# Block transposes of x on VectorE and score products on sixteen array tiles

## The chip, the cores and the metric

The kernel runs on one core of a Trainium2 chip. The metric is the device time of one execution in microseconds (us), with lower being better; the time of a kernel is the median of several executions.

## The reference

Inputs are `x` (8 batches, 8 heads, 512 tokens, 64 features) and `state` (8 batches, 8 heads, 32 states, 64 features), both float32, and the float64 weights of a gated feed-forward layer. For every batch and head, tokens read from states and states read from tokens; the 512 + 32 rows of each batch, with the heads side by side, are then 544 rows of 512 features for the layer.

```python
scale = 1.0 / np.sqrt(D)
scores = scale * np.matmul(x, state.transpose(0, 1, 3, 2))
a = softmax(scores)                       # max subtracted; sum + 1e-9
xread = np.matmul(a, state)
scores2 = scale * np.matmul(state, x.transpose(0, 1, 3, 2))
a2 = softmax(scores2)
sread = np.matmul(a2, x)
rows = concatenate([xread, sread], axis=2)     # then (B*(S+Ns), H*D)

xn = rows / sqrt(mean(rows**2) + 1e-6) * rms_g
g = xn @ w_gate                                # 512 -> 1536
out = (g * sigmoid(g) * (xn @ w_val)) @ w_out  # 1536 -> 512
```

`scores2` is the transpose of `scores`, so one set of score products serves both reads.

## The kernel before, in words

**Reading (attention).** `tokens_read(b)` makes, for batch b, the weights with which tokens read states. The state of a batch lies packed in `rows`, 128 partitions of four pairs of heads times 32 states, and x in `x_b`, 128 tokens on the partitions in four chunks. TensorE turns both round with an identity (L268 for the state, L278 for x: 16 transposes of 128 by 128), VectorE copies the state's transpose out (L271) and ScalarE that of x, chunk by chunk (`xT`, L280). The score products at L287 have 64 rows (the features of one head), 32 columns of weights (its states) and 512 tokens: eight of them on eight tiles of the array, the even heads into one bank of the PSUM pool `at`, the odd ones into the other. VectorE turns the scores in blocks of 32 by 32 (L298, `eS`), takes the maximum over the states (L307), subtracts it (L309), ScalarE takes the exponential (L311), VectorE sums, divides and turns back (L318 to L325), which gives `aT_s`. ScalarE also copies the scores as they are (`sS`, L300) for `states_read(b)`, which makes the states' reads from them (L368 to L406). A product of `aT_s` with the state (L332), squares (L339), sums (L342, L346) and a power on GpSimd give the normalization of each token, and L356 scales `aT_s` by it. The tokens' reads themselves are never written: the layer's weights are multiplied by the state once for each batch (`own_weights`, L450, copied out at L461), so that the hidden layer's products take `aT_s` directly.

**The layer.** Batch 0 uses plain products (`hidden`, L492, and `project_as_ready`, L690), in step with the weights as they become ready. Batches 1 to 7 and the states use seven block products for eight (`hidden_seven`, L596; `project_seven`, L750), with sums on VectorE and GpSimd.

**The weights** come as float64, four pieces ahead (`raws`), and are turned into float32 by three ScalarE steps (L195 to L200) and four VectorE steps (L221 to L233); 18 pieces, all in the stage of batch 0. Pairs of them are stored in HBM (`w_d`) and fetched again for every batch (L148).

**Order.** The work of TensorE, VectorE and ScalarE is laid down by hand, in strings in which each letter advances one stream by one step: `ORDER` for batch 0 with the reading of batches 0 and 1, the weights and batch 0's layer; `PERIOD` for each of batches 1 to 7, with the reading of the next batch within it; `STATES` for the rows of the states. In `ORDER`, a and A are the tokens' reads of batches 0 and 1, s and S the states' reads, e and d the weights' ScalarE and VectorE steps, v the weights by the state, h, t, u the hidden layer and p its projection. In `PERIOD`, a and s are the reading of the next batch. Engines work through their instructions in this order. The DMA queues have the order in which the loads and stores are issued, nearly all on the sync queue (SPq); batch 0's x is shared between that queue and ScalarE's.

PSUM has two buffers each of `at` and `pv` for these steps; the layer has four banks of its own.

Of the kernel before, what the change touches and what calls it, by code (L numbers as in the profile page):

```python
# [8 lines left out]
F32 = mybir.dt.float32  # L9
# [10 lines left out]
W_BUFS = 3  # L20

ORDER = (
    "aaaaaaaaddaaaaaaeaseeaasadsassssdsaaaasaeadesaeeasdasaaeadeadaaaddeeasedaadsadae"
    "edvvavdadeaAhdeeddtdAdAAhueheAeedtddphAedvdvduvdphedeAedtdhApeehddeuAdddeAhdedvd"
    "tudvvpeAAAAdhdAAteAehuhpddephepdeAdAeApAdteedAAvvveAdpudAAephtdSdhAdphdeAueedhAd"
    "eAteudddeeSppAddAAdppAdAdevApvdveehhAdthAudhpdeddeedeAdteAupvdvdvphedAAtdShhutSA"
    "hpukSSSkkkwSwkpSkpwpSSckSScckkpcSwkkkwwww"
)

PERIOD = (  # L30
    "hthtvvhhtuxxhuhthuhththuuhtuuhhxxhhuvxutvhtthuuhuhthuuxhxhxuxtthuhuthhuthuxxhuta"
    "uahatuhtaxuuuhtauahuahhaahuttuhutauhhhtuuahuhuutauphuauupuauapacasapaaaapapaskaa"
    "aaksacccassppakckpaaackasaapakapaskaaaswpksksswsxxwxxpxcspcskx"
)

STATES = (
# [6 lines left out]
def kernel(  # L43
# [31 lines left out]
    SCALE = 1.0 / D ** 0.5  # L75
# [3 lines left out]
    one = ctx.enter_context(tc.tile_pool(name="one", bufs=1))  # L79
    two = ctx.enter_context(tc.tile_pool(name="two", bufs=2))  # L80
# [3 lines left out]
    aps = ctx.enter_context(tc.tile_pool(name="aps", bufs=2, space=PSUM))  # L84
    vps = ctx.enter_context(tc.tile_pool(name="vps", bufs=2, space=PSUM))
# [9 lines left out]


    rows = {}
    x_sb = {}

    def load_state(b):  # L100

        rows[b] = two.tile([P, 2, D], F32, name="rows")
        for j in range(4):
            src = state[b, 2 * j:2 * j + 2].rearrange("e n d -> n e d")
            nc.sync.dma_start(out=rows[b][Ns * j:Ns * j + Ns], in_=src)

    def load_x(b, *queues):
        x_sb[b] = two.tile([P, NC, H * D], F32, name="x_b")
        for c in range(NC):
            (queues or (nc.sync,))[c % max(1, len(queues))].dma_start(  # L110
                out=x_sb[b][:, c].rearrange("p (h d) -> p h d", h=H),
                in_=x[b, :, P * c:P * c + P, :].rearrange("h p d -> p h d"))

    ident = consts.tile([P, P], F32, name="ident")
    make_identity(nc, ident)
# [7 lines left out]
    rms_g = consts.tile([P, NI], F32, name="rms_g")  # L123
# [119 lines left out]
    stT_g = {}  # L243
    aT_s = {}
# [16 lines left out]
    read = {}  # L261

    def tokens_read(b):
        xb, packed = x_sb[b], rows.pop(b)
        stT = two.tile([P, 4, Ns], F32, name="stT")
        stT_g[b] = two.tile([P, 4, Ns], F32, name="stT_g")
        tp = aps.tile([P, 4, Ns], F32, name="at")
        TE.transpose(out=tp.rearrange("p j n -> p (j n)"),  # L268
                     in_=packed.rearrange("p e d -> p (e d)"), identity=ident)
        yield  # L270
        VE.tensor_copy(stT, tp)  # L271
        yield "step"

        xT = one.tile([P, 4, NC, P], F32, name="xT", tag="xT")
        for c in range(NC):
            tp = aps.tile([P, 4, P], F32, name="at")
            for j in range(4):
                TE.transpose(out=tp[:, j, :], in_=xb[:, c, P * j:P * j + P], identity=ident)  # L278
            yield
            SE.copy(xT[:, :, c, :], tp)  # L280
            yield "step"


        sp = [aps.tile([P, S], F32, name="at") for e in range(2)]
        for j in range(4):
            for e in range(2):
                TE.matmul(out=sp[e][Ns * j:Ns * j + Ns, :], lhsT=stT[D * e:D * e + D, j, :],  # L287
                          rhs=xT[D * e:D * e + D, j].rearrange("p c t -> p (c t)"),
                          start=True, stop=True)
        yield  # L290


        sS = read[b] = two.tile([P, 2, NC, P], F32, name="sS")
        eS = one.tile([P, 2, S // Ns, Ns], F32, name="eS", tag="eS")
        m1 = two.tile([P, 2, S // Ns], F32, name="m1")
        z1 = two.tile([P, 2, S // Ns], F32, name="z1")
        for e in range(2):
            VE.transpose(out=eS[:, e].rearrange("p k n -> p (k n)"), in_=sp[e])  # L298
            yield
            SE.copy(sS[:, e].rearrange("p c t -> p (c t)"), sp[e])  # L300
            yield "step" if e else None

        def along(t, e):
            return t[:, e].unsqueeze(2).to_broadcast([P, S // Ns, Ns])

        for e in range(2):
            VE.reduce_max(out=m1[:, e], in_=eS[:, e], axis=AXX)  # L307
            yield
            VE.tensor_tensor(out=eS[:, e], in0=eS[:, e], in1=along(m1, e), op=ALU.subtract)  # L309
            yield  # L310
            SE.activation(out=eS[:, e], in_=eS[:, e], func=ACTF.Exp, scale=SCALE)  # L311
            yield "step"
        VE.tensor_tensor(out=stT_g[b], in0=stT, in1=rms_g.unsqueeze(2).to_broadcast([P, 4, Ns]),
                         op=ALU.mult)
        yield
        aT_s[b] = two.tile([P, 2, S], F32, name="aT_s")
        for e in range(2):
            VE.reduce_sum(out=z1[:, e], in_=eS[:, e], axis=AXX)  # L318
            yield
            VE.tensor_scalar(z1[:, e], z1[:, e], 1e-9, None, op0=ALU.add)  # L320
            VE.reciprocal(z1[:, e], z1[:, e])
            yield
            VE.tensor_tensor(out=eS[:, e], in0=eS[:, e], in1=along(z1, e), op=ALU.mult)
            yield
            VE.transpose(out=aT_s[b][:, e], in_=eS[:, e].rearrange("p k n -> p (k n)"))  # L325
            yield "step"


        reads = [(aps, vps)[j // 2].tile([P, S], F32, name=("at", "pv")[j // 2]) for j in range(4)]
        for j in range(4):  # L330
            for e in range(2):
                TE.matmul(out=reads[j][D * e:D * e + D, :],  # L332
                          lhsT=packed[Ns * j:Ns * j + Ns, e, :],
                          rhs=aT_s[b][Ns * j:Ns * j + Ns, e],
                          start=True, stop=True)
        yield
        sq = one.tile([P, 4, S], F32, name="sq", tag="xT")
# [12 lines left out]
        VE.tensor_scalar(ss, sp, 1e-6, None, op0=ALU.add)  # L350
        yield "step"
        ri = mean_root(ss, NC)
        yield
        rp = along_rows(ri, NC)
        yield
        VE.tensor_tensor(out=aT_s[b], in0=aT_s[b],  # L356
                         in1=rp.unsqueeze(1).to_broadcast([P, 2, S]), op=ALU.mult)
        yield "step"

    def states_read(b):  # L360

        xb, sS = x_sb.pop(b), read.pop(b)
        e2 = one.tile([P, 2, NC, P], F32, name="e2")
        s2 = two.tile([P, 2], F32, name="s2")
        m2 = two.tile([P, 2], F32, name="m2")
        z2 = two.tile([P, 2], F32, name="z2")
        for e in range(2):
            VE.reduce_max(out=m2[:, e:e + 1], in_=sS[:, e].rearrange("p c t -> p (c t)"),  # L368
                          axis=AXX)
            yield  # L370
        VE.tensor_scalar(s2, m2, -SCALE, None, op0=ALU.mult)
        yield
        for e in range(2):
            SE.activation(out=e2[:, e], in_=sS[:, e], func=ACTF.Exp, scale=SCALE,
                          bias=s2[:, e:e + 1], accum_out=z2[:, e:e + 1])
            yield "step" if e else None
        e2T = one.tile([P, 2, NC, P], F32, name="e2T")
        for e in range(2):
            tp = aps.tile([P, NC, P], F32, name="at")
# [9 lines left out]
        for e in range(2):  # L389
            for c in range(NC):  # L390
                for j in range(4):
                    h = 2 * j + e
                    TE.matmul(out=rp[Ns * j:Ns * j + Ns, e, :],  # L393
                              lhsT=e2T[:, e, c, Ns * j:Ns * j + Ns],
                              rhs=xb[:, c, D * h:D * h + D],
                              start=(c == 0), stop=(c == NC - 1))
# [511 lines left out]
    n = B * (NM // 2)  # L908
# [37 lines left out]
```

## Time and profile before

| | |
|---|---|
| time, median of 3 | 802.42 us (801.93 to 803.89) |
| span of the profiled execution | 800.7 us |
| TensorE busy | 775.7 us, 97% |
| VectorE busy | 515.1 us, 64% |
| ScalarE busy | 347.0 us, 43% |
| GpSimd busy | 178.0 us, 22% |
| TensorE on the transposes of x (L278) | 21.0 us, 128 instructions |
| TensorE on the score products (L287) | 8.7 us, 128 instructions |
| ScalarE on the copies of x's transpose (L280) | 18.8 us, 32 instructions |
| moved by DMA | 94.11 MB, 117 GB/s from and to HBM over the span |

In the profile PE is TensorE's products, PEld its loading of weights, DVE VectorE, ACT ScalarE, POOL GpSimd, SPq the sync engine's queue of DMA issues. The page cuts the span in 40 slices of about 20 us and gives the busy share of each in tenths. A group's line names source line, engine, operation, output and inputs, shapes and count; after the first bar stand total busy time (us) and mean duration of one (ns), after the second the idle time just before them and what ended it. Durations of products overlap, so the mean of one is more than its share of the busy time. The chain of waits is followed back from the last instruction to what released each, and its pieces tell how long each group held the end back.

### The profile page before, as it was taken

How to read it: one execution, taken by the hardware profiler on the slowest of the kernel's cores; microseconds unless marked ns; L12 is line 12 of the kernel's file. 1: busy time of each engine (PE TensorE's matmuls, PEld its weight loads, DVE VectorE, ACT ScalarE, POOL GpSimd, SP SyncE). 2: the span in 40 equal slices, each digit the busy share in tenths (PEclk: the TensorE clock that was granted, in tenths of full speed). 3: DMA queues.
4: the chain of work that ended last, by engine and by line, in shares of the span. 5: the costliest groups of instructions: out<-in, count | busy, mean ns of one | idle time of the engine just before them, and what ended most of it. 6: DMA issues, size and time to landing. Idle time of an engine off the chain costs nothing.

```text
span 800.7 us, 12112 instructions
## 1 busy us (share of the span) xinstructions
PE 775.7 (97%) x4822; PEld 594.2 (74%) x4822; DVE 515.1 (64%) x786; ACT 347.0 (43%) x572; POOL 178.0 (22%) x215
## 2 busy tenths in 40 slices
PE   4599999999999999999999999999999999999998
PEld 3244444788778887888778887888788877888996
DVE  5989997588337852786358833785178735891461
ACT  5888864553145323543256314532354224510320
POOL 0000003530155004510443015500451044400000
PEclk8599999999999999999999999999999999999999
DMA  9888745710182007400361018200540024101311
GB/s 295 245 264 308 263 161 172 251 53 0 36 284 106 1 16 214 194 1 15 116 232 63 1 34 285 106 1 14 179 177 2 13 107 178 71 0 46 113 54 27
DMA packets 61592, 94.11 MB, mean 118 GB/s; under 512 B 38752, under 2 KB 46432, under 8 KB 54624
## 3 DMA queue, kind: packets, MB, share of 16 engines
q1 hardware_dynamic: 59360, 92.75, 33.5%
q8 instruction: 38, 0.62, 0.3%
q10 hardware_dynamic: 2176, 0.59, 0.3%
q14 instruction: 18, 0.15, 0.1%
HBM read 78.12 MB, written 15.20 MB: 117 GB/s over the span
## 4 chain that ended last, share of the span: by engine, by line
PE 94%; DVE 4%; ACT 1%; issue 0%; DMA 0%; SPq 0%; DVEq 0%
PE f L596 37%; PE f L750 35%; PE f L690 5%; PE pv L492 4%; PE at L450 3%; PE pv L450 3%; PE at L278 2%; PE at L332 1%; PE at L287 1%; PE at L346 1%; PE at L393 1%; PE at L381 1%; DVE ex L228 1%; DVE raw L224 1%; PE at L257 1%; DVE w_m L233 0%
## 5 line engine op out<-in xcount | busy, mean ns | idle before, releaser
L750 PE MATMUL f<-wo,hb 128*128 128x256 f32 x540 | 124.2, 382 | 0.4 <-ACT ot L787 0.2
L658 DVE TENSOR_TENSOR g<-g,f 128x512 f32<-128x512 f32 (+1 forms) x96 | 62.8, 654 | 90.0 <-PE f L596 86.6
L596 PE MATMUL f<-aT_s,v 128*128 128x256 f32 x504 | 119.5, 380 | 0.0
L750 PEld LDWEIGHTS f<-wo,hb 128*128 128x128 f32 x540 | 101.4, 190 | 20.1 <-ACT ot L787 6.9
L596 PEld LDWEIGHTS f<-aT_s,v 128*128 128x128 f32 x504 | 93.8, 190 | 17.4 <-issue 5.2
L250 POOL TENSOR_TENSOR ri<-ss,mhalf 128x4 f32<-128x4 f32 x8 | 9.1, 1142 | 364.7 <-DVE ss L350 364.7
L596 PE MATMUL f<-aT_t,vs 128*128 128x256 f32 x336 | 87.2, 382 | 0.0
L750 PE MATMUL f<-wt,hs 128*128 128x256 f32 x360 | 80.4, 379 | 0.0
L649 ACT ACTIVATE hb<-g 128x1024 f32<-128x1024 f32 (+1 forms) x48 | 48.2, 1004 | 63.0 <-DVE g L658 63.0
L750 PEld LDWEIGHTS f<-wt,hs 128*128 128x128 f32 x360 | 68.3, 190 | 9.5 <-issue 0.2
L787 ACT COPY ot<-f 128x256 f32<-128x256 f32 x60 | 21.5, 371 | 122.5 <-PE f L750 122.5
L596 PEld LDWEIGHTS f<-aT_t,vs 128*128 128x128 f32 x336 | 62.6, 190 | 15.1 <-issue 5.9
L661 DVE SCALAR_TENSOR_TENSOR hb<-hb,g 128x1024 f32<-128x1024 f32 x42 | 55.5, 1322 | 7.8 <-ACT hb L649 7.8
L647 ACT COPY g<-f 128x512 f32<-128x512 f32 (+1 forms) x48 | 26.9, 561 | 76.7 <-PE f L596 76.7
L479 POOL TENSOR_TENSOR vs<-v,vs 128x256 f32<-128x256 f32 x42 | 58.4, 1390 | 0.0
L476 POOL TENSOR_TENSOR vs<-v 128x256 f32<-128x256 f32 x42 | 30.6, 729 | 118.4 <-ACT v L461 118.4
L492 PE MATMUL pv<-aT_s,v 128*128 128x512 f32 x96 | 46.2, 623 | 1.1 <-DVE aT_s L356 1.1
L690 PE MATMUL f<-wo,hb 128*128 128x512 f32 x96 | 44.7, 600 | 0.0
L596 PE MATMUL f<-aT_t,v 128*128 128x256 f32 x168 | 43.9, 383 | 0.0
L596 PE MATMUL f<-aT_s,vs 128*128 128x256 f32 x168 | 43.1, 379 | 0.0
L750 PE MATMUL f<-wt,hb 128*128 128x256 f32 x180 | 42.6, 386 | 0.0
L750 PE MATMUL f<-wo,hs 128*128 128x256 f32 x180 | 41.6, 382 | 0.0
(128 smaller groups left out, 1237.2 us busy)
## 6 DMA issues: line engine op xcount, KB each, us to landing
w_m<-w_d SPq DMA_DIRECT2D x48, 1024.0 KB, 6.7
x_b<-in_x_dram SPq DMA_DIRECT2D x30, 256.0 KB, 4.2
out_dram<-ot SPq DMA_DIRECT2D x56, 128.0 KB, 1.8
raw<-in_moe_w_val_dram SPq DMA_DIRECT2D x6, 1024.0 KB, 5.2
raw<-in_moe_w_out_dram SPq DMA_DIRECT2D x6, 1024.0 KB, 7.2
w_d<-w_m SPq DMA_DIRECT2D x6, 1024.0 KB, 4.9
raw<-in_moe_w_gate_dram SPq DMA_DIRECT2D x5, 1024.0 KB, 5.8
raw<-in_moe_w_gate_dram SPq DMA_DIRECT2D x2, 512.0 KB, 4.9
```

The lines of the kernel that those rows point to most:

```text
L450: TE.matmul(out=pv[e][Ns * j:Ns * j + Ns, :], lhsT=stT_g[b][D * e:D * e + D, j, :], rhs=w[D * e:D * e + D, j].rearrange("p m k f -> p (m k ...
L476: GE.tensor_tensor(out=vs[:, 0], in0=a21, in1=a22, op=ALU.add)
L479: GE.tensor_tensor(out=vs[:, 2], in0=a12, in1=vs[:, 1], op=ALU.subtract)
L492: TE.matmul(out=to[0], lhsT=lhs(i, k), rhs=r, start=(i == 0), stop=(i == len(rhs) - 1))
L596: TE.matmul(out=ps[:, i, 0:half], lhsT=l[:, i, :], rhs=r, start=(start and i == 0 and k == 0), stop=(k == len(lhs) - 1), skip_group_check= ...
L647: SE.copy(gates(q)[1], q["x"][:, :, 0:half])
L649: SE.activation(out=hb[:, 2 * mp:2 * mp + 2, 0:n].rearrange("p m (c t) -> p m c t", c=2), in_=q["g"][:, :, :, 0:half], func=ACTF.Silu if s ...
L658: VE.tensor_tensor(out=to, in0=to, in1=q[ps][:, :, 0:half], op=ALU.add)
L661: VE.scalar_tensor_tensor(out=h, in0=h, scalar=1.0, op0=ALU.add, op1=ALU.mult, in1=q["g"].rearrange("p m c t -> p m (c t)"))
L690: TE.matmul(out=banks[r], lhsT=hb[:, m, P * r:P * r + P], rhs=wo[:, m, :], start=(m == 0), stop=(m == NM - 1))
L750: TE.matmul(out=banks[name][:, r, :], lhsT=lhs(k)[:, P * r:P * r + P], rhs=rhs(k), start=(start and r == 0 and k == 0), stop=(k == HM - 1) ...
L787: SE.copy(to, banks[name][:, r, :])
```

## The change

VectorE transposes in blocks of 32 by 32 take the place of TensorE's transposes of x and of their copies by ScalarE. For this x is loaded so that the 32-partition group g of a tile holds the tokens 128 g to 128 g + 127, 32 of them in each chunk. A block transpose then puts 32 features on the partitions of each group, and the 64 features of a head become two halves, k = 0 and 1, one after the other in the free dimension. The state is needed on all four groups with the same halves, so it is loaded a second time, four-fold (`fours`), and turned by VectorE as well (`stB`).

The score products then have 32 rows (half a head's features), 32 columns of weights and 128 tokens; the two halves accumulate. Token group g sets the rows of the array, pair of heads j the columns, so that sixteen tiles are in use; each group g writes a bank of its own, four in all, two from `at` and two from `pv`. What follows works on token groups (four pieces, in two halves) where it worked on even and odd heads. The packed state's transpose by TensorE stays for the weights' scaling (`stT_g`), which now reads it from PSUM. `ORDER` and `PERIOD` are new; `STATES` stays.

The aim is to take the transposes off TensorE and the copies off ScalarE.

```diff
 def load_state(b):
+        fours[b] = one.tile([P, H, D], F32, name="fours")
+        for g in range(4):
+            nc.sync.dma_start(out=fours[b][Ns * g:Ns * g + Ns],
+                              in_=state[b].rearrange("h n d -> n h d"))

 def load_x(b, *queues):
         x_sb[b] = two.tile([P, NC, H * D], F32, name="x_b")
-        for c in range(NC):
-            (queues or (nc.sync,))[c % max(1, len(queues))].dma_start(
-                out=x_sb[b][:, c].rearrange("p (h d) -> p h d", h=H),
-                in_=x[b, :, P * c:P * c + P, :].rearrange("h p d -> p h d"))
+        for i in range(4 * NC):
+            c, g = divmod(i, 4)
+            (queues or (nc.sync,))[i % max(1, len(queues))].dma_start(
+                out=x_sb[b][Ns * g:Ns * g + Ns, c].rearrange("p (h d) -> p h d", h=H),
+                in_=x[b, :, P * g + Ns * c:P * g + Ns * c + Ns, :].rearrange("h p d -> p h d"))

 def tokens_read(b):
-        VE.tensor_copy(stT, tp)
-        for c in range(NC):
-            tp = aps.tile([P, 4, P], F32, name="at")
-            for j in range(4):
-                TE.transpose(out=tp[:, j, :], in_=xb[:, c, P * j:P * j + P], identity=ident)
-            SE.copy(xT[:, :, c, :], tp)
-        sp = [aps.tile([P, S], F32, name="at") for e in range(2)]
-        for j in range(4):
-            for e in range(2):
-                TE.matmul(out=sp[e][Ns * j:Ns * j + Ns, :], lhsT=stT[D * e:D * e + D, j, :],
-                          rhs=xT[D * e:D * e + D, j].rearrange("p c t -> p (c t)"),
-                          start=True, stop=True)
-        for e in range(2):
-            VE.transpose(out=eS[:, e].rearrange("p k n -> p (k n)"), in_=sp[e])
-            SE.copy(sS[:, e].rearrange("p c t -> p (c t)"), sp[e])
+        VE.transpose(out=stB.rearrange("p h k n -> p (h k n)"),
+                     in_=fours.pop(b).rearrange("p h d -> p (h d)"))
+        n = NC if b == 0 else 2
+        for i in range(n):
+            c = slice(NC // n * i, NC // n * i + NC // n)
+            VE.transpose(out=xB[:, c].rearrange("p c h k t -> p (c h k t)"),
+                         in_=xb[:, c].rearrange("p c f -> p (c f)"))
+        sp = [(aps, vps)[g // 2].tile([P, 2, NC, Ns], F32, name=("at", "pv")[g // 2])
+              for g in range(4)]
+        for e in range(2):
+            for k in range(2):
+                for j in range(4):
+                    for g in range(4):
+                        TE.matmul(out=sp[g][Ns * j:Ns * j + Ns, e].rearrange("n c t -> n (c t)"),
+                                  lhsT=stB[Ns * g:Ns * g + Ns, 2 * j + e, k, :],
+                                  rhs=xB[Ns * g:Ns * g + Ns, :, 2 * j + e, k, :],
+                                  start=(k == 0), stop=(k == 1), skip_group_check=True)
+        for g in (2, 3, 0, 1):
+            VE.transpose(out=eS[:, g].rearrange("p e c n -> p (e c n)"),
+                         in_=sp[g].rearrange("p e c t -> p (e c t)"))
+            SE.copy(sS[:, :, :, g, :], sp[g])
...
-        VE.tensor_tensor(out=stT_g[b], in0=stT, in1=rms_g.unsqueeze(2).to_broadcast([P, 4, Ns]),
+        VE.tensor_tensor(out=stT_g[b], in0=tp, in1=rms_g.unsqueeze(2).to_broadcast([P, 4, Ns]),
                          op=ALU.mult)
...
-            VE.transpose(out=aT_s[b][:, e], in_=eS[:, e].rearrange("p k n -> p (k n)"))
+            for g in (2 * q, 2 * q + 1):
+                VE.transpose(out=aT_s[b][:, :, P * g:P * g + P],
+                             in_=eS[:, g].rearrange("p e c n -> p e (c n)"))
```

In the changed kernel's own line numbers the new transposes stand at L272 (state) and L280 (x), the products at L292, the turned scores at L305, their copies at L308, the scaling of `aT_s` at L374.

More of the change, by code (lines that the diff above doesn't have):

```diff
@@ L22 @@
 ORDER = (
[L23 to L27, printed above, removed]
+    "aaaaeaaaadaaaaaaasessesadaesassadaaasaeesdadasaaaesddaaeseaadddadaaaeaeaedsasdea"
+    "vdaddeAveaavddeehhdtdudheAtddehpepedvevvduAAddAdeAddeAAeddhpethdhAeeddpthAdAeAev"
+    "eupvvAudAdhAhpteedAdhpddAeepdAAeduhdptdpeAededvAAuevvddAdpdAeepdedhthhAedudAhptA"
+    "eeAuedAedpApdddAAAdevpvvAAdehehdtddhAeAupddeddheddteAApeuvvSdpAvhSedddhthuShtSAp"
+    "ukkSkkSwSkSSwkSpppSSkpwkcScSwckckkkwwww"
 )
 PERIOD = (
-    "hthtvvhhtuxxhuhthuhththuuhtuuhhxxhhuvxutvhtthuuhuhthuuxhxhxuxtthuhuthhuthuxxhuta"
-    "uahatuhtaxuuuhtauahuahhaahuttuhutauhhhtuuahuhuutauphuauupuauapacasapaaaapapaskaa"
-    "aaksacccassppakckpaaackasaapakapaskaaaswpksksswsxxwxxpxcspcskx"
+    "hhtvhthxtxuhuhhtxhtuuhathhtuuhvuuvxathhxxhuhththuxtuhuuuxhhhtutathhuuthuhuhhvxut"
+    "uhhutuhutuxuxthhuxuhtuaaahhattuhuhtuuhhuhuuuaapahptauuacuuaasaaaaassaaasaapaskpa"
+    "apkssapcussppacccaacaapkskpsakaakapaakaawspswkxswpxkxxcxpxkc"
 )
@@ L97 @@
     rows = {}
+    fours = {}
     x_sb = {}
@@ L264, in tokens_read @@
         xb, packed = x_sb[b], rows.pop(b)
-        stT = two.tile([P, 4, Ns], F32, name="stT")
+        stB = one.tile([P, H, 2, Ns], F32, name="stB")
+        VE.transpose(out=stB.rearrange("p h k n -> p (h k n)"),
+                     in_=fours.pop(b).rearrange("p h d -> p (h d)"))
+        yield
+        xB = one.tile([P, NC, H, 2, Ns], F32, name="xB", tag="xT")
+        n = NC if b == 0 else 2
[3 more added lines that the diff above has]
+                         in_=xb[:, c].rearrange("p c f -> p (c f)"))
+            yield
@@ new lines, in tokens_read @@
+        yield
+        sS = read[b] = two.tile([P, 2, NC, 4, Ns], F32, name="sS")
+        eS = one.tile([P, 4, 2, NC, Ns], F32, name="eS", tag="eS")
+        m1 = two.tile([P, 2, 4 * NC], F32, name="m1")
+        z1 = two.tile([P, 2, 4 * NC], F32, name="z1")
+        for g in (2, 3, 0, 1):
+            VE.transpose(out=eS[:, g].rearrange("p e c n -> p (e c n)"),
+                         in_=sp[g].rearrange("p e c t -> p (e c t)"))
+            yield
+            SE.copy(sS[:, :, :, g, :], sp[g])
+            yield "step" if g == 1 else None
@@ new lines, in half, with along @@
+        def half(q):
+            return eS[:, 2 * q:2 * q + 2].rearrange("p g e c n -> p (g e c) n")
+        def along(t, q):
+            return t[:, q].unsqueeze(2).to_broadcast([P, 4 * NC, Ns])
+        for q in range(2):
+            VE.reduce_max(out=m1[:, q], in_=half(q), axis=AXX)
+            yield
+            VE.tensor_tensor(out=half(q), in0=half(q), in1=along(m1, q), op=ALU.subtract)
+            yield
+            SE.activation(out=half(q), in_=half(q), func=ACTF.Exp, scale=SCALE)
+            yield "step"
@@ L270, in tokens_read @@
         yield
-        VE.tensor_copy(stT, tp)
-        yield "step"
-        xT = one.tile([P, 4, NC, P], F32, name="xT", tag="xT")
-        for c in range(NC):
-            tp = aps.tile([P, 4, P], F32, name="at")
-            for j in range(4):
[L278 to L281, printed above, removed]
-        sp = [aps.tile([P, S], F32, name="at") for e in range(2)]
-        for j in range(4):
-            for e in range(2):
-                TE.matmul(out=sp[e][Ns * j:Ns * j + Ns, :], lhsT=stT[D * e:D * e + D, j, :],
-                          rhs=xT[D * e:D * e + D, j].rearrange("p c t -> p (c t)"),
-                          start=True, stop=True)
[L290 to L296, printed above, removed]
-        for e in range(2):
-            VE.transpose(out=eS[:, e].rearrange("p k n -> p (k n)"), in_=sp[e])
-            yield
-            SE.copy(sS[:, e].rearrange("p c t -> p (c t)"), sp[e])
[L301 to L312, printed above, removed]
-        VE.tensor_tensor(out=stT_g[b], in0=stT, in1=rms_g.unsqueeze(2).to_broadcast([P, 4, Ns]),
+        VE.tensor_tensor(out=stT_g[b], in0=tp, in1=rms_g.unsqueeze(2).to_broadcast([P, 4, Ns]),
                          op=ALU.mult)
@@ L316, in tokens_read @@
         aT_s[b] = two.tile([P, 2, S], F32, name="aT_s")
-        for e in range(2):
-            VE.reduce_sum(out=z1[:, e], in_=eS[:, e], axis=AXX)
+        for q in range(2):
+            VE.reduce_sum(out=z1[:, q], in_=half(q), axis=AXX)
             yield
-            VE.tensor_scalar(z1[:, e], z1[:, e], 1e-9, None, op0=ALU.add)
-            VE.reciprocal(z1[:, e], z1[:, e])
+            VE.tensor_scalar(z1[:, q], z1[:, q], 1e-9, None, op0=ALU.add)
+            VE.reciprocal(z1[:, q], z1[:, q])
             yield
-            VE.tensor_tensor(out=eS[:, e], in0=eS[:, e], in1=along(z1, e), op=ALU.mult)
+            VE.tensor_tensor(out=half(q), in0=half(q), in1=along(z1, q), op=ALU.mult)
             yield
-            VE.transpose(out=aT_s[b][:, e], in_=eS[:, e].rearrange("p k n -> p (k n)"))
+            for g in (2 * q, 2 * q + 1):
+                VE.transpose(out=aT_s[b][:, :, P * g:P * g + P],
+                             in_=eS[:, g].rearrange("p e c n -> p e (c n)"))
             yield "step"
@@ L367, in states_read @@
         for e in range(2):
-            VE.reduce_max(out=m2[:, e:e + 1], in_=sS[:, e].rearrange("p c t -> p (c t)"),
+            VE.reduce_max(out=m2[:, e:e + 1], in_=sS[:, e].rearrange("p c g t -> p (c g t)"),
                           axis=AXX)
@@ L373, in states_read @@
         for e in range(2):
-            SE.activation(out=e2[:, e], in_=sS[:, e], func=ACTF.Exp, scale=SCALE,
+            SE.activation(out=e2[:, e], in_=sS[:, e].rearrange("p c g t -> p c (g t)"), func=ACTF.Exp, scale=SCALE,
                           bias=s2[:, e:e + 1], accum_out=z2[:, e:e + 1])
```

## The prediction

> **What bounds the kernel now.** I read four views in turn. First the page's busy shares, slices and chain of waits:
>
> ```profile
> PE 775.7 (97%) x4822; PEld 594.2 (74%) x4822; DVE 515.1 (64%) x786; ACT 347.0 (43%) x572; POOL 178.0 (22%) x215
> ...
> PE   4599999999999999999999999999999999999998
> ...
> DVE  5989997588337852786358833785178735891461
> ...
> PE 94%; DVE 4%; ACT 1%; issue 0%; DMA 0%; SPq 0%; DVEq 0%
> ```
>
> TensorE carries 94% of the chain and is full from the third slice (40 us) on. VectorE is full only in the first six slices (to 120 us), where the weights are turned from float64 to float32; later it has room. The busy times of five windows sharpen this; after the window's limits and length come busy time and instruction count of PE, PEld, DVE, ACT, POOL, then clock, DMA share, GB/s:
>
> ```profile
> 44.00:64.00 20.00, 19.77 (x83) 8.38 (x81) 18.96 (x20) 17.23 (x21) 0.00 (x0) 1.00 0.86 293
> 64.00:100.00 36.00, 36.00 (x128) 14.73 (x125) 35.59 (x47) 30.39 (x35) 0.00 (x0) 1.00 0.80 287
> 100.00:110.00 10.00, 10.00 (x38) 4.01 (x37) 9.54 (x12) 8.19 (x11) 0.00 (x0) 1.00 0.64 216
> 110.00:121.00 11.00, 11.00 (x47) 4.89 (x46) 9.79 (x12) 5.73 (x7) 1.16 (x1) 1.00 0.23 96
> ```
>
> From 44 to 100 us TensorE and VectorE are both full: work added to VectorE there is not free. A busy TensorE need not run at its peak, so I price its work by what the chain of waits gives each group, start to next start. The chain between 240 and 300 us, in one batch of the steady part (start, us, what):
>
> ```profile
> 256.04 0.44 PE at L278 x4
> 256.47 1.73 PE f L596 x8
> 258.20 0.44 PE at L278 x4
> ...
> 266.43 1.02 PE at L287 x16
> 267.45 1.92 PE f L596 x8
> ```
>
> Four transposes of x (L278) hold TensorE for 0.44 us, the score products (L287) for 1.02 us; neighbours follow without a gap. Last, the groups by shape:
>
> ```profile
> L278 PE MATMUL at<-ident,x_b 128*128 128x128 f32 x128 | 21.0, 296 | 0.0
> L393 PE MATMUL at<-x_b,e2T 128*32 128x64 f32 x512 | 9.4, 228 | 0.0
> L287 PE MATMUL at<-xT,stT 64*32 64x512 f32 x128 | 8.7, 601 | 0.7 <-ACT xT L280 0.7
> L325 DVE STREAM_TRANSPOSE aT_s<-eS 128x512 f32<-128x512 f32 x16 | 11.4, 710 | 0.8
> ```
>
> A float32 product shows as two instructions: 64 score products are x128. L325 is VectorE's 32 by 32 transpose from SBUF, 710 ns for 512 columns.
>
> **What the Trainium skill says.** "TensorE: Matmul & The Clock Gate", Part 3, gives products on separate 32 by 32 tiles a span of one product's duration plus about 4 ns for each further tile, and 10.6 times on sixteen. No run so far has sixteen tiles; L393 (four column tiles) supports the concurrency: six batches hold TensorE 6.60 us for 384 instructions after 160 us, 17.2 ns each, though one lasts 228 ns. Part 1 of that page gives a floor of about 25 ns from start to start; L393 lies under it, so I don't take it. "TensorEngine Tiling (Array Packing)", Performance Considerations, warns that the packing doesn't speed up emptying PSUM; here the emptying is VectorE and ScalarE work that I cost below. "VectorE: DVE Perf Modes", The three transpose paths, says that VectorE transposes only within 32 by 32 blocks; L325 is of that kind, and its 710 ns is my price.
>
> **The change part by part.**
> 1. *TensorE loses* the transposes of x: 16 a batch, 4 x 0.44 = 1.76 us, straight off the path for batches 2 to 7. Batch 1's lie between 41 and 64 us, mostly in the warm clock, again about 1.8. Batch 0's run before 9.2 us, where TensorE waits anyway. The packed state's transpose stays, only later.
> 2. *Score products*: before, 8 a batch on eight tiles, 1.02 us. After, 64 of 32 rows and 128 columns, 128 instructions on sixteen tiles. Array time: one L287 instruction holds its tile for half of (1.02 - 0.17) = 0.43 us for 512 columns (0.17 is duration 0.60 less 0.43), so 0.107 us for 128 columns; each tile gets 8, which makes 0.85 us, and 0.17 for the fill: 1.02, the lower end. Upper end: L393's 17.2 ns x 128 = 2.2 us, if starting them is what limits. L393 itself is nearly bound by its array (64 columns take 53 ns, 13 ns on four tiles), so its 17.2 overstates the cost of a start; at the skill's 4 ns each for load and product, 128 pairs take 1.0 us beside the array's time. I take 1.3. So +0.28 a batch, and a net 1.76 - 0.28 = 1.48 us saved; batches 2 to 7: 6 x 1.48 = 8.9 us (6 x 0.58 = 3.5 at the upper end of products, 10.6 at the lower).
> 3. *VectorE gains*, per batch: transposing the four-fold state 0.71; x in two of 1024 columns at about 1.22 (row L356 has that size), 2.45; scores and weights in eight pieces of 256 columns (nearest row of that size: 0.42) for four of 0.71, +0.5; less the copy of stT, 0.29. Sum 3.4 us, about 27 us in all, to 542. In five windows of 100 us from 200 to 700 us VectorE is busy 57 to 65 us, and with periods of some 88 us gains 4; I cost it at nothing there, since TensorE's row hides it.
> 4. *ScalarE loses* four copies of 0.59 a batch and copies the scores in four of 0.37 instead of two of 0.58: about -2 us a batch, off the path, worth nothing after 64 us.
> 5. *Loads.* The x of a batch goes from 4 to 16 issues, the state from 4 to 8. Later they have a queue with slack. At the start they don't; this is the timeline of the sync queue before (start, length, issue):
>
> ```profile
> 0.74 1.78 SPq L105 DMA_DIRECT2D rows<-in_state_dram  x4
> 2.56 1.06 SPq L110 DMA_DIRECT2D x_b<-in_x_dram  x2
> 3.83 0.99 SPq L859 DMA_DIRECT2D rms_g<-in_moe_rms_g_dram  x1
> 4.86 1.25 SPq L166 DMA_DIRECT2D raw<-in_moe_w_gate_dram  x2
> ```
>
> An issue costs 0.45 to 0.53 us whatever its size. The changed kernel's order has 4 more state loads and 6 more x loads there (8 of x instead of 2), so the last x issue ends at 3.62 + 10 x 0.48 = 8.4 us and the first raw weights are issued at about 10 instead of 5. A state load landed 2.95 us after its issue: the last block of x is there at about 11, its transpose ends at 11.7, the products end at 13.0 to 13.8. Before, VectorE turned the scores at 10.99. That is **+2.5 us**. Behind it waits the whole of batch 0 on VectorE: in the chain it runs without a gap from 11.0 to 23.9 us. VectorE's first two weight steps (0.43 + 0.70, at 9.46 us) ran in the shadow of that wait and now come after the scores: +1.1. Four pieces instead of two, twice, +0.5, and the state of batch 1, put ahead of the scaling of aT_s in the new order, +0.7. So batch 0's weights, scaled at L356 at 36.4 to 37.6 us before, come **4.8 us later**, and TensorE's solid row begins that much later.
> 6. *From there to 130 us.* TensorE has less to do: batch 1's transposes gone, its products dearer, -1.5. If it stays full, the stage ends 4.8 - 1.5 = 3.3 us later. VectorE has 4.8 + 2.4 (x of batch 1) + 0.5 - 0.3 = 7.4 us more, against gaps of 2.1 us at 42.7 (waiting for hb's first product), 0.5 between 100 and 110 and 1.2 between 110 and 121: 3.6 net. The two agree closely; I take **+3.3**.
>
> Sum: 802.4 + 3.3 - 8.9 = **796.8 us**.
>
> New waits: the score products need all four banks of the pools at and pv at once, so behind them on TensorE queue the hidden layer's products until ScalarE has copied earlier weights out (0.6 us each). In the orders other work stands between; from 200 to 700 us TensorE is idle 0.2 us in all before, and I expect little more. The single buffer of the four-fold state makes the sync queue hold batch b+2's load until VectorE has turned batch b+1's; the new period puts that step early, so the weight fetches behind it are not held past their use.
>
> **Rivals.**
> - *The start hides its own losses.* The clocks and gaps before 41 us leave TensorE under half used, and the new order may place weight steps where I count a delay. For it: +2.5 us rests on issues of 0.48 us that may overlap the two queues better. Against: VectorE is in the chain for nearly all of 11 to 24 us. Then the start costs 0 and batch 1's saving counts: 802.4 - 8.9 - 1.5 = 792.0 us.
> - *The small products are bound by their starts, and the start slips further.* 2.2 us a batch leaves 0.58 saved, 3.5 in all; raw weights landing at 15 us rather than 13 hold VectorE, whose second score step stands behind the first weight step, so the start costs about 6. 802.4 + 6 - 3.5 = 804.9 us, slower. For: no row has 32-row tiles. Against: L393's concurrency.
> - *Small products dear, start as forecast*: 802.4 + 3.3 + 0.9 - 3.5 = 803.1, no change (0.9: batch 1's own).
> - *VectorE becomes the later bound.* At up to 69% and with digits up to 8 in single slices its waits could reach TensorE; at 1 us a period this would add 7 and end at 804. The row of 9s under DVE digits of 8 speaks against it.
>
> **How the numbers follow.** Forecast 0.53, start hidden 0.22, dear products without a slip 0.08, dear with slip 0.11, VectorE 0.06. Faster than 800.0: the first two and a little of the third, 0.77; within 0.3%: the rest of the third and most of the last, 0.11; slower than 804.8: 0.12. The range reaches from just under the hidden start, with the products at their lower end (790.5), to the case of no change (803); what lies outside is about 0.18.
>
> **What will show it.** Right: the group L278 gone; the new product group holding TensorE 1.0 to 1.6 us a batch on the chain; TensorE's busy time down by 12 to 15 us, to about 761 to 764; VectorE near 542, ScalarE near 331; scores first turned at 13 to 14 us; L374 (the scaling of aT_s) of batch 0 ending near 42; TensorE's idle time after 64 us still a few us. Wrong: products at 2 us or more a batch, gaps on TensorE of over 1 us a period released by VectorE or by banks, or a start whose scaling of aT_s comes at 38 or at 46 us.

## The result and the profile after

The changed kernel takes 812.97 us (median of 4) against 802.21 us beside it: 1.013 times as long, 95% interval 1.0112 to 1.0148. The forecast was 796.8 us with a range of 790.5 to 803.0: wrong in sign, by 16 us.

The page of the changed kernel, the rows that answer to those shown before (busy times; slices of PE and DVE; the chain of waits by engine):

```profile
PE 767.9 (95%) x5590; PEld 589.5 (73%) x5590; DVE 529.5 (65%) x836; ACT 335.0 (41%) x558; POOL 165.1 (20%) x215
...
PE   1589999999999999999999999999999999999998
...
DVE  4999996789338861787358933886187734792461
...
PE 89%; DVE 7%; ACT 2%; issue 1%; DMA 1%; SPq 1%; DVEq 0%
```

TensorE's busy time fell by 7.8 us, where 12 to 15 were forecast, while the span grew by 10.4. So TensorE waits more: its share of the chain is down from 94% to 89%. Two places are visible at once, the first slice (4 tenths before, 1 now) and, in the list of TensorE's waits (who waited for whom: us in all, times, longest), the second of these lines:

```profile
PE at L292 <- DVE xB L280: 11.9, 1, 11.9
PE f L768 <- ACT ot L805: 9.2, 6, 1.5
PE at L399 <- ACT e L392: 4.9, 1, 4.9
PE at L350 <- DVE aT_s L342: 3.9, 1, 3.9
```

The first, third and fourth line are the start. The second has almost no counterpart in the kernel before:

```profile
PE f L750 <- ACT ot L787: 0.2, 1, 0.2
```

Now it comes six times, once in each period that also reads a next batch: TensorE stands 1.5 us before a projection product.

To part start and periods I take from the timeline of TensorE the start of the first projection product of batch 1 (L750 before, L768 after), and that of each later batch. Batch 1's, before and after:

```profile
182.31 1.89 PE L750 MATMUL f<-wo,hb 128*128 128x256 f32 x8
```

```profile
187.72 1.46 PE L768 MATMUL f<-wo,hb 128*128 128x256 f32 x6
```

Batch 2's stand at 269.21 and 275.35 us. A period thus takes 86.90 us before and 87.63 after. Of the 10.4 us of span, 5.4 are there at batch 1's first projection. The other 5.0 come later: 0.73 in each of the five periods up to batch 6's mark, where a saving of 1.5 was forecast, and 1.57 in the one after it, which has the wait, but had no next transposes that could be saved.

How each period loses them is seen in the timeline of the changed kernel from 298 to 301 us (start, length, engine, line, tiles; in brackets the idle time before and what ended it):

```profile
298.12 0.37 ACT L805 COPY ot<-f 128x256 f32<-128x256 f32 x1 [4.05 <-PE f L768]
298.50 0.61 PE L350 MATMUL at<-aT_s,rows 32*64 32x512 f32 x4
...
299.26 1.08 ACT L357 ACTIVATE sq<-pv 128x512 f32<-128x512 f32 x2 [0.76 <-PE pv L350]
300.23 0.38 ACT L805 COPY ot<-f 128x256 f32<-128x256 f32 x1
...
300.66 5.45 PE L768 MATMUL f<-wo,hb 128*128 128x256 f32 x24 [1.53 <-ACT ot L805]
```

ScalarE copies the first half of a projection bank at 298.12. The second half could follow at 298.5, but in the new PERIOD two squares of the tokens' reads (L357) stand between the two copies, and they need the reads (L350) that TensorE has just begun. ScalarE waits 0.76 us for the reads, squares for 1.08 us, and only then copies; TensorE's next product adds into the copied bank and waits 1.53 us.

The score products of the same period in the chain of waits (start, us, what):

```profile
262.06 5.38 PE f L614 x24
267.44 0.23 PE at L292 x2
...
269.24 0.03 PE pv L292 x2
269.27 6.24 PE f L614 x28
```

They hold TensorE from 267.44 to 269.27, 1.83 us, against 1.02 for the eight large products. The transposes and their 1.76 us are gone, so the saving on the chain is 1.76 - 0.81 = 0.95 us a batch, not 1.48.

### The profile page after: what moved, and what is told of

Its sections match the earlier page's. It is cut to its first block, busy times and chain, and to the rows that moved or that the text cites. A ratio compares the mean times of both kernels' runs of the same rounds, so it can differ in the third digit from the quotient of the medians.

```text
span 811.1 us, 13856 instructions
## 1 busy us (share of the span) xinstructions
PE 767.9 (95%) x5590; PEld 589.5 (73%) x5590; DVE 529.5 (65%) x836; ACT 335.0 (41%) x558; POOL 165.1 (20%) x215
## 4 chain that ended last, share of the span: by engine, by line
PE 89%; DVE 7%; ACT 2%; issue 1%; DMA 1%; SPq 1%; DVEq 0%
PE f L614 37%; PE f L768 34%; PE pv L510 3%; PE at L468 3%; PE f L708 3%; PE pv L468 2%; DVE raw L230 1%; DVE ex L234 1%; PE at L292 1%; PE at L350 1%; ACT sq L357 1%; PE at L364 1%; PE at L411 1%; PE pv L292 1%; PE at L399 1%
## 5 line engine op out<-in xcount | busy, mean ns | idle before, releaser
L768 PE MATMUL f<-wo,hb 128*128 128x256 f32 x540 | 123.3, 380 | 9.2 <-ACT ot L805 9.2
L768 PEld LDWEIGHTS f<-wo,hb 128*128 128x128 f32 x540 | 101.5, 190 | 27.7 <-ACT ot L805 14.5
L768 PE MATMUL f<-wt,hs 128*128 128x256 f32 x360 | 80.4, 379 | 0.0
L768 PEld LDWEIGHTS f<-wt,hs 128*128 128x128 f32 x360 | 67.4, 190 | 9.3 <-issue 0.2
L494 POOL TENSOR_TENSOR vs<-v 128x256 f32<-128x256 f32 x42 | 33.2, 790 | 153.2 <-ACT v L479 152.7
L479 ACT COPY v<-pv 128x512 f32<-128x512 f32 x42 | 24.0, 589 | 87.2 <-PE pv L468 84.8
L360 DVE TENSOR_TENSOR sq<-sq 128x512 f32<-128x512 f32 x24 | 16.5, 689 | 40.7 <-ACT sq L357 40.3
L676 DVE TENSOR_TENSOR c<-c,f 128x512 f32<-128x512 f32 (+1 forms) x48 | 31.3, 653 | 16.5 <-PE f L614 16.5
L768 PE MATMUL f<-wt,hb 128*128 128x256 f32 x180 | 42.0, 383 | 0.0
```

The source lines that it names most:

```text
L479: SE.copy(v[:, e].rearrange("p m k f -> p (m k f)"), pv[e])
L494: GE.tensor_tensor(out=vs[:, 0], in0=a21, in1=a22, op=ALU.add)
L676: VE.tensor_tensor(out=to, in0=to, in1=q[ps][:, :, 0:half], op=ALU.add)
L768: TE.matmul(out=banks[name][:, r, :], lhsT=lhs(k)[:, P * r:P * r + P], rhs=rhs(k), start=(start and r == 0 and k == 0), stop=(k == HM - 1) ...
```

## The experiments

First two repairs and a test of the size of the products, then the start.

**e1_c_early**: one letter of PERIOD moves.

```diff
-    "apkssapcussppacccaacaapkskpsakaakapaakaawspswkxswpxkxxcxpxkc"
+    "apkssapcussppaccccaaaapkskpsakaakapaakaawspswkxswpxkxxcxpxkc"
```

> The changed kernel with one letter of PERIOD moved: ScalarE's copy of the last quarter of the second product to be kept (ot, L805) stands ahead of the first two squares (L357) instead of behind them. In the changed kernel TensorE stands 1.53 us in each of six periods at L768 waiting for that copy. Theory (the wait is only the order of ScalarE's instructions): the wait goes, 6 x 1.53 = 9.2 us, about 803.8 us, period 86.1 us instead of 87.6. Rival (TensorE is held there by something else as well, the banks of the reads or the squares themselves): the idle time turns up at the next product or at L364, and the time stays within 2 us of 813.

Measured 803.27 us (median of 20; ratio to before 1.0007, interval 1.0001 to 1.0014), 9.7 us less than the changed kernel. The period is 86.04 us. In the chain of e1 the reads and the next product now follow without a piece of ScalarE between them:

```profile
297.63 0.40 PE at L350 x4
298.03 0.03 PE pv L350 x4
298.06 5.38 PE f L768 x24
```

The wait was only the order of ScalarE's instructions. With it gone the kernel's time is about that of the kernel before: what the periods save, 0.86 us each, pays for the later start.

**e2_load4**: x in four issues a batch; the last transpose spreads its result instead.

```diff
-        for i in range(4 * NC):
-            c, g = divmod(i, 4)
-            (queues or (nc.sync,))[i % max(1, len(queues))].dma_start(
-                out=x_sb[b][Ns * g:Ns * g + Ns, c].rearrange("p (h d) -> p h d", h=H),
-                in_=x[b, :, P * g + Ns * c:P * g + Ns * c + Ns, :].rearrange("h p d -> p h d"))
+        for c in range(NC):
+            (queues or (nc.sync,))[c % max(1, len(queues))].dma_start(
+                out=x_sb[b][:, c].rearrange("p (h d) -> p h d", h=H),
+                in_=x[b, :, P * c:P * c + P, :].rearrange("h p d -> p h d"))
...
-                VE.transpose(out=aT_s[b][:, :, P * g:P * g + P],
-                             in_=eS[:, g].rearrange("p e c n -> p e (c n)"))
+                VE.transpose(out=aT_s[b].rearrange("p e (c g n) -> p g e c n", g=4, n=Ns)[:, g],
+                             in_=eS[:, g])
```

> The changed kernel with x loaded as before: four issues of 128 partitions for a batch instead of sixteen of 32; the chunk's tokens are again 128 c to 128 c + 127, and the last transpose (L342) writes each piece to its tokens with a stride instead. Theory (the issues and their queueing make most of the loss at the start, 5.4 us at the first projection of batch 1): first turned scores about 2 us earlier (12.5 us instead of 14.9), total 2 to 4 us less, 809 to 811 us. Rival (VectorE's added work makes it, and later periods don't care): under 1 us less, 812 to 813. A second rival: the strided transposes cost VectorE more than before and the time rises.

Measured 811.67 us (ratio 1.0114, interval 1.0098 to 1.0129): 1.3 less than the changed kernel, between the two expectations (e1 and e5, which differ by the same edit, are 0.9 apart). The first scores are turned at 12.88 instead of 14.84 us and aT_s is scaled at 39.43 instead of 41.39, so the issues of x cost 2.0 us at the first scores, where the forecast had 2.5 for these and the state's together. They are not the most of the loss.

**e3_split64**: each score product cut in two of 64 tokens.

```diff
-                        TE.matmul(out=sp[g][Ns * j:Ns * j + Ns, e].rearrange("n c t -> n (c t)"),
-                                  lhsT=stB[Ns * g:Ns * g + Ns, 2 * j + e, k, :],
-                                  rhs=xB[Ns * g:Ns * g + Ns, :, 2 * j + e, k, :],
-                                  start=(k == 0), stop=(k == 1), skip_group_check=True)
+                        for q in range(2):
+                            c = slice(2 * q, 2 * q + 2)
+                            TE.matmul(out=sp[g][Ns * j:Ns * j + Ns, e, c].rearrange("n c t -> n (c t)"),
+                                      lhsT=stB[Ns * g:Ns * g + Ns, 2 * j + e, k, :],
+                                      rhs=xB[Ns * g:Ns * g + Ns, c, 2 * j + e, k, :],
+                                      start=(k == 0 and q == 0), stop=(k == 1), skip_group_check=True)
```

> The changed kernel with each score product cut in two of 64 tokens: 256 instructions a batch instead of 128, the same array time. They hold TensorE 1.83 us a batch in the changed kernel, 14.3 ns an instruction; the array's own time is 0.85 us. Theory (the products are bound by their starts, with the loading of their weights): 3.6 us a batch, 8 x 1.8 = 14 us more, about 827 us. Rival (bound by the array, or by tiles that don't run beside each other): the products stay near 1.9 us and the time within 2 us of 813.

Measured 846.37 us (ratio 1.0543, interval 1.0519 to 1.0567). The busy times of the score products alone between 310 and 400 us, one batch, in the changed kernel and then in e3 (limits and length, PE, PEld, clock, DMA share, GB/s):

```profile
310.00:400.00 90.00, 1.90 (x128) 1.53 (x128) 1.00 0.30 100
```

```profile
310.00:400.00 90.00, 3.69 (x256) 3.37 (x256) 1.00 0.29 98
```

That is 14.8 ns an instruction of 128 tokens, 14.4 of 64: the number of instructions decides, not the tokens in each. Every product comes with a weight load (PEld, 1.53 and 3.37 us in these lines); which of the two sets the pace is not parted here. The time rose by 33 us, though, not by the 14 that follow from 8 x 1.8. TensorE's waits in e3 say where part of the rest is:

```profile
PE pv L294 <- issue: 11.7, 5, 3.7
PE at L294 <- DVE xB L280: 11.1, 2, 9.8
...
PE at L294 <- issue: 3.2, 3, 1.6
```

In the midst of the products TensorE stands for 1 to 4 us with nothing to wait for, 14.9 us in all. Why was not found, and some 4 us stay unexplained.

**e4_hybrid**: batches 0 and 1 as before, batches 2 to 7 as changed, with both repairs.

```diff
+        if b < 2:
+            return
         fours[b] = one.tile([P, H, D], F32, name="fours")
...
-    streams = {"a": tokens_read(0), "s": states_read(0), "A": tokens_read(1), "S": states_read(1),
+    streams = {"a": tokens_read_early(0), "s": states_read(0), "A": tokens_read_early(1), "S": states_read(1),
```

`tokens_read_early` is the reading of the kernel before, and ORDER is that of the kernel before.

> Batches 0 and 1 read as in the kernel before, with its ORDER and no four-fold state for them; batches 2 to 7 read as in the changed kernel, with x loaded in four issues, its PERIOD and the moved letter. Theory (loss = start 5.4 + six waits of 1.53, against a saving of 1.76 - 0.81 = 0.95 us a batch): start as before, six periods of 86.1 instead of 86.9 us, 802.2 - 6 x 0.8 = 797.4 us. Rival (VectorE's work or the four banks cost the later periods as well): between 800 and 804 us.

Measured 797.36 us (ratio 0.9937, interval 0.992 to 0.9953): faster than both kernels. Its first projection of batch 1 stands at 181.06 us and its period is 86.03. Against this kernel the changed one starts 187.72 - 181.06 = **6.7 us late**, and that is the loss of the start at this mark; against the kernel before it shows as 5.4, in the main because batch 2's cheaper reading (0.95 us) lies ahead of the mark. By the times the start costs less: e1, with the same PERIOD, takes 803.27 - 797.36 = 5.9 us more than the hybrid. A time holds more than the profiled span, and in the hybrid this rest is 0.7 us longer (797.32 against a span of 794.8; e1 803.85 against 802.0).

**e5_both**: the changed kernel with e1 and e2 together.

> The changed kernel with both repairs: x loaded in four issues a batch, and the copy moved ahead of the squares in PERIOD. Theory (the two losses are separate): 803.3 - 1.3 = 802.0 us, the loads having brought 1.3 us by the times and the letter 9.7; so no difference from the kernel before (802.4). Rival (the earlier start is eaten by a later wait): 803 us or more.

Measured 802.35 us (ratio 0.9995, interval 0.9987 to 1.0004), no difference from before. The two losses add, and what remains, 5.0 us over the hybrid, is the start (first projection at 187.09; the period is 86.03, as in the hybrid).

One profile's mark is not exact, however. e2 and e5 have the same instructions up to it and stand at 185.69 and 187.09. All of these 1.4 us come from the first sixteen products of batch 0's hidden layer, e2's and then e5's:

```profile
40.66 8.68 PE L509 MATMUL pv<-aT_s,v 128*128 128x512 f32 x16 [1.41 <-DVE aT_s L373]
```

```profile
40.54 10.21 PE L509 MATMUL pv<-aT_s,v 128*128 128x512 f32 x16 [1.41 <-DVE aT_s L373]
```

Why the same products ran slower once was not found. The granted clock that the profile records does not say it: from 42 to 64 us it is 0.96 in e2 and 1.00 in e5. Nor is that clock the changed kernel's loss: its profile has 0.92 there, e1's with the same start 1.00, and e1's mark is no earlier (188.24). Differences of marks below 1.4 us are therefore not read in what follows.

**e6_j_inner**: e5 with the rows of the array outside and the columns inside.

```diff
-                for j in range(4):
-                    for g in range(4):
+                for g in range(4):
+                    for j in range(4):
```

> As e5_both, but the score products go through the pairs of heads j (columns of the array) innermost and the token groups g (rows) outside, so that four neighbours use the same rows. Question: what sets the 14.3 ns from start to start. Theory (the plain rate at which pairs of weight load and product are taken in): the same 1.83 to 1.90 us a batch, about 802 us. Rival (a weight load can run ahead of a product only on other rows): products of 2.5 us a batch or more, 5 us or more in all.

One run: 802.1 us. The products between 310 and 400 us take as long as with the other order:

```profile
310.00:400.00 90.00, 1.90 (x128) 1.52 (x128) 1.00 0.33 105
```

Whether neighbours use the same rows or other ones does not set the 14 to 15 ns.

**e7_dve**: the hybrid with four idle block transposes on VectorE in batch 1's reading.

```diff
+        if b == 1:
+            spare = one.tile([P, H, D], F32, name="spare", tag="fours")
...
             SE.copy(xT[:, :, c, :], tp)
+            if b == 1:
+                VE.transpose(out=spare.rearrange("p h d -> p (h d)"), in_=xb[:, c])
```

> As e4_hybrid (797.4 us), with four more block transposes of 512 columns on VectorE, whose result nobody reads, in the reading of batch 1, where the changed kernel turns x: 2.8 us of VectorE's time between 45 and 75 us. Theory (VectorE is co-bound while it turns the weights, so its added work is not hidden there): 1.5 to 2.8 us more, 799 to 800 us. Rival (hidden beside TensorE): under 0.5 us more.

Measured 798.96 us (ratio 0.9953, interval 0.9938 to 0.9968), 1.6 more than the hybrid for 2.8 us of added VectorE time. The first projection of batch 1 moves by 2.1 us, 0.35 of which stand ahead of the added work (aT_s is scaled at 37.62 instead of 37.27). TensorE's waits between 42 and 130 us show the way, in the hybrid and then in e7:

```profile
PE at L536 <- DVE w_m L240: 0.3, 1, 0.3
```

```profile
PE at L540 <- DVE w_m L240: 1.3, 1, 1.3
```

The weights come later, and the product that needs them waits. More than half of VectorE's added time in this stage is not hidden.

**e8_new_from_1**, **e9_new1_old_order**, **e10_old_new_order** part the rest of the start: batch 0 read as before in all three; batch 1 read new or old, in the changed ORDER or the one before.

```diff
-    "aaaaeaaaadaaaaaaasessesadaesassadaaasaeesdadasaaaesddaaeseaadddadaaaeaeaedsasdea"
+    "aaaaaaaadaaaaaaeasessesadaesassadaaasaeesdadasaaaesddaaeseaadddadaaaeaeaedsasdea"
...
-    streams = {"a": tokens_read(0), "s": states_read(0), "A": tokens_read(1), "S": states_read(1),
+    streams = {"a": tokens_read_early(0), "s": states_read(0), "A": tokens_read(1), "S": states_read(1),
```

This is e8 against the changed kernel, the beginning of ORDER and the streams. e10 has the same ORDER as e8, e9 that of the kernel before. Both read batch 1 by a `tokens_read_second` of their own: in e10 the old reading on the places of the new one, in e9 the new reading on the places of the old one.

> As e5_both, but batch 0 alone is read as in the kernel before (TensorE's transposes, eight products), with the changed ORDER, in which one ScalarE weight step is moved behind the reading's first steps. It parts the loss at the start, which is 4.6 us at the first projection of batch 1 between e2_load4 and e4_hybrid. Theory (the most of it is batch 0's longer way to its scores: 3.0 us at the scaling of aT_s): 802.0 - 3.0 = 799 us. Rival (the most is batch 1's added VectorE work and products): 800.5 us or more.

> As e4_hybrid (797.4 us, ORDER of the kernel before), but batch 1 is read the new way, its steps laid on the places of the old ones. Against e8_new_from_1 (801.1 us, the changed ORDER) it parts the reading of batch 1 from the order around it. Theory (the reading itself costs: VectorE's work, dear as e7_dve showed, and four banks held at once): 800 us or more. Rival (the changed ORDER costs): VectorE's 3 us cost about 2 and TensorE's saving brings back 1, so 798 to 799 us.

> As e8_new_from_1, but batch 1 too is read as in the kernel before, inside the changed ORDER, its steps laid on the places of the new ones. Theory (the reading of batch 1 costs): back to about 797.5 us. Rival (the changed ORDER costs, whichever way the batches are read): 800 us or more.

| batch 1 read | ORDER before | ORDER changed |
|---|---|---|
| as before | e4: 797.36 us, first projection at 181.06 | e10: 802.72 us, 187.05 |
| new | e9: 801.49 us, 186.40 | e8: 801.06 us, 185.86 |

Neither theory holds alone. The expectation of e8 fell: putting batch 0 back won 1.3 us (802.35 to 801.06), not 3. Against the hybrid, the new reading of batch 1 in the old order costs 4.1 us by the times (5.3 at the mark) and the old reading in the new order 5.4 (6.0), but both together 3.7 (4.8), so the two costs do not add. Part of this may be that in e9 and e10 the steps were laid on places made for others; no run tests it. What is shown is that the best start known pairs old reading with old ORDER, that neither order brought a new reading of batch 1 below a median of 801 us, and that VectorE's added time alone can account for about 2 us of the loss (e7: 1.6 by the times). The share of the ORDER itself stays open.

In the changed kernel the start shows one further kind of wait, which the new products bring with them. TensorE's timeline at batch 1's score products:

```profile
56.38 0.78 PE L292 MATMUL at<-xB,stB 32*32 32x128 f32 x3 [0.73 <-ACT v L479]
...
59.69 1.13 PE L510 MATMUL pv<-aT_s,v 128*128 128x512 f32 x2 [0.93 <-ACT sS L308]
```

All four banks are needed at once: the products wait 0.73 us for a bank that ScalarE empties (v, L479), and the hidden layer's next product waits 0.93 us for ScalarE's copy of the scores (sS, L308). The same two lines are in e5 and e8. In the later periods neither appears.

## Why the prediction was wrong, point by point

- **Point 1, the transposes**, was right: the 1.76 us a batch left the chain.
- **Point 2, the score products**, was mis-sized: 1.83 us instead of 1.3, 6 x 0.53 = 3.2 us. The step that failed is the choice of about 4 ns for a start, from the Trainium skill ("TensorE: Matmul & The Clock Gate", Part 3). That page gives it for each further tile; that a weight load costs no more was the prediction's own addition. e3 shows 14.4 ns for a pair of weight load and product, close to the 17.2 ns of L393, which the prediction had put aside. Its upper end of 2.2 us did hold for batches 2 to 7 (batch 1's products took 2.29 us, batch 0's 2.82), as did leaving aside the 25 ns floor of the same page's Part 1.
- **"I expect little more" of TensorE's waits** failed, and it is the largest term: 6 x 1.53 = 9.2 us. The fourth bullet of the rivals thought of VectorE as the later bound; it was ScalarE, which the change relieves, and not its load but the place of one copy behind two squares. The prediction looked at the banks at and pv; it did not follow the layer's banks, whose copies the new PERIOD places anew. The row of 9s it relied on was a row of the old order.
- **Points 5 and 6, the start.** The scaling of aT_s begins at 41.39 us (36.42 before), 5.0 us later where 4.8 was forecast, but that is luck, two errors that cancel: the first scores were turned at 14.84 us, not at 13.0 to 13.8, since batch 0's products alone took 2.8 us, and behind them 1.1 us was added where 2.3 was forecast. (Its "whatever its size" for an issue does not fit rms_g's 0.99 us in its own view, but the sync queue's eight issues of x came as counted, in 3.76 us.) The step that failed is the next one, "TensorE has less to do: -1.5", for a net of 3.3. In its place the start ends 6.7 us late at the mark, 5.9 by the times. TensorE stood idle 3.2 us from 42 to 130 us, against 0.2 before; 0.6 of these are the rest of the wait for aT_s. What the runs show at work there is VectorE's added time (e7: 1.6 to 2.1 us for 2.8), the waits for four banks (0.73 and 0.93 us) and 2.29 us for batch 1's products; how the loss divides among these and the new ORDER stays open. The prediction set VectorE's gaps, 3.8 us, against 7.4 us of its work; in e7 at most 1.2 of 2.8 us were taken up so.
- **Points 3 and 4, the other engines.** ScalarE's 335.0 us is near the forecast 331; VectorE's 529.5 is below the 542. Its new transposes of x and state take 26 us, as priced. Most of the difference is a group that the change leaves alone, before and after:

```profile
L669 DVE SCALAR_TENSOR_TENSOR hb<-hb,c 128x512 f32<-128x512 f32 x42 | 40.5, 965 | 1.4
```

```profile
L687 DVE SCALAR_TENSOR_TENSOR hb<-hb,c 128x512 f32<-128x512 f32 x42 | 31.6, 753 | 1.2
```

Its 42 instructions take 753 ns each in the hybrid too, which shares the new PERIOD; why was not found, and no time is known to hang on it.

Sum of the misses at the marks: 9.2 + 3.2 + (6.7 - 3.3) = 15.8 of the 16.2 us; by the times, 9.7 (e1) + 3.2 + (5.9 - 3.3) = 15.5. The direction of the forecast per batch was right in the mechanism, as e4 shows: 6 x 0.87 = 5.2 us are to be had, once the start is left alone and the copy is in its place.

## What to carry to other kernels

When a change comes with a new hand-made order, read the order as part of the change: for each in-order engine look for an instruction that frees a buffer and stands behind one that has yet to be fed, since one such place costs its wait in every period. Work moved off the bound engine is free only in the stages where the receiving engine has room; here a start in which both are full was better left as it was. Price many small products by the measured interval of the nearest small products, not by their array time.

## What the runs showed of the hardware that was not expected

- Float32 products on sixteen tiles of 32 rows by 32 columns, each with a weight load of its own, started every 14 to 15 ns on average, for 64 and for 128 tokens, whichever of rows and columns ran inside (e3, e6). For L292 that is 1.83 us on the chain where the array's own time was worked out at 0.85. The 4 ns that the Trainium skill gives for each further tile was not seen here, with a weight load for every product.
- With 256 such instructions a batch TensorE stood for 1 to 4 us without a recorded cause; with 128, in the changed kernel, no such stand is among its waits.
- Loads in flight held up the sync queue behind them. The changed kernel's queue from batch 1's four-fold state on (start, length):

```profile
15.13 10.04 SPq L109 DMA_DIRECT2D fours<-in_state_dram  x4
25.22 7.86 SPq L116 DMA_DIRECT2D x_b<-in_x_dram  x16
33.19 0.39 SPq L172 DMA_DIRECT2D raw<-in_moe_w_val_dram  x1
```

From its list of waits, what the first of these waited for:

```profile
SPq L109 <- DMA raw<-in_moe_w_gate_dram: 3.5, 2, 3.0
SPq L109 <- DMA raw<-in_moe_w_out_dram: 3.5, 1, 3.5
SPq L109 <- DMA raw<-in_moe_w_val_dram: 2.3, 1, 2.3
```

Four issues of 64 KB took 10 us, and for 9.3 of these the profile names weight loads ahead of them that had not landed. The kernel before has such a place too, six issues of x in 11.11 us at 10.80. The fifth piece of weights was issued at 33.19 us instead of 25.22: 4.8 of these 8.0 us because VectorE was done with the first piece later (at 30.00 instead of 25.16), the rest because batch 1's sixteen issues of x stood ahead of it.
